# Last block of a fused attention and two-MLP kernel: six tiles of 512 tokens in place of eight of 384, its second product transposed, its buffers laid out anew

## The chip, the cores and the metric

The kernel runs on one core of one Trainium2 chip. The metric is the device time of one execution in microseconds (us). TensorE's clock has two levels, 1.2 and 2.4 GHz; the profile gives the granted level as a share of the higher one (PEclk, 1.0 or 0.5).

## The reference, cut to what matters

Four sequences of 768 tokens, eight heads of 48, pass a linear recurrence with complex decays; its output, 3072 tokens by 384, passes two feed-forward blocks. Only the second of these, the last block, is changed:

```
def _moe_ref(x, w1, w2, w3, w_out):      # 384 -> 1024 -> 384
    return ((x @ w1) * (x @ w2) @ w3) @ w_out

def _moe2_ref(x, w_in, w_out):           # 384 -> 2048 -> 384
    h = x @ w_in
    sp = np.where(h > 20.0, h, np.log1p(np.exp(np.minimum(h, 20.0))))
    g = h * np.tanh(sp)
    return (g @ w_out).astype(np.float32)
```

Everything is float32. On the chip each factor of a large product is split into two float32r parts, hi + lo (`split`: a cast on ScalarE and a subtraction on VectorE), and a product is three matmuls: hi by hi, and the two mixed ones (`mm3`, L464).

## The kernel before, in words

**Ahead of the last block.** The recurrence is done in chunks of 96 tokens, and the first feed-forward block in eight tiles of 384 tokens (`TT`, L28) as generators that `_merge` interleaves (L566 to L579). The first block's result for tile `i` goes to DRAM, transposed, as `x2_d[i]` of 128 x 3 x 384: at the end of `m1_stream` each of three PSUM banks is copied to the buffer `x2`, of which there is one (`bufs=1`, L510), and stored from there (L511, L512). The last tile, `m1_stream(7)`, is drained by itself at L591.

**The last block.** Tokens stay in eight tiles of 384. For each tile and each of 16 slices `f` of the 2048 hidden units:

- `hid` (L601): nine matmuls of 384 columns give the hidden slice in PSUM (128 hidden units by 384 tokens). The stationary operands are the parts of `w_in` (`wih`, `wil`), the moving ones the parts of the tile's input (`x2h`, `x2l`). ScalarE takes sigmoid(-h) to `wb`, VectorE copies h to `hb`. Five PSUM banks go round.
- `soft` (L613): over groups of slices (8 of them, fewer in the first and the last tile), a maximum on VectorE and a logarithm on ScalarE, with a table load ahead of it and one behind it.
- `mish` (L619): for two slices at a time, tanh, the product with `hb`, and the split into `gh` and `gl` (three buffers of each).
- `fin` (L630): nine matmuls accumulate the output of the tile in three PSUM banks. The stationary operands are 128 tokens of `gh` or `gl`, the moving ones a slice of `w_out` (`wuh`, `wul`, 384 columns); a bank holds 128 tokens by 384 outputs.

The loop at L662 runs over all (tile, slice) pairs: `mish` comes 10 steps and `fin` 13 steps behind `hid`, so that in the middle a `hid` and a `fin` of nine matmuls each alternate on TensorE. A tile's input is loaded and split by `x2_load` at slice 8 of the tile before (L676). The first tile's input is loaded at L590, ahead of the last tile of the first block, into buffers of the pool `mp`, which both blocks share; `w_out` comes in 16 slices (`wor`) in the first 16 steps.

The program's order on each engine comes from a scheduler that keeps dependencies; a tile in a buffer that another tile held waits until that one's last reader and its transfers are done. A pool that is opened in the place of closed pools inherits such waits from all that lay there.

```
590    x2_load(0)
591    _drain(m1_stream(NTILE - 1))
592    ph1.close()
594    gp = ph2.enter_context(tc.tile_pool(name="gp", bufs=2))
```

Of the kernel before, what the change touches and what calls it, by code (L numbers as in the profile page):

```python
# [10 lines left out]
F32 = mybir.dt.float32  # L11
# [17 lines left out]
NTILE = NT // TT  # L29
BLK = 7  # L30
EM20 = float(np.exp(-20.0))
# scaled by 2**-112, a float64's leading word holds the float32's exponent; this is the last in its range
# [27 lines left out]
def kernel(  # L60
# [46 lines left out]
    stg = ctx.enter_context(tc.tile_pool(name="stg", bufs=2, side="right"))  # L107
# [7 lines left out]
    # |a| has to lie between 0.75 and 1e4 for the chunked form: 1/|a| within LR of LC  # L115
# [9 lines left out]
    def decode(src, n, dst=None, pool=None, bufs=None, cap=False, signs=False):  # L125
        """float64 words of DRAM to float32 on chip, cut to 24 bits; values out of range are flagged or capped."""
        raw = (pool or stg).tile([128, n, 2], I32, tag="raw64", name="raw64", bufs=bufs)
        if len(src.shape) == 3:
            nc.sync.dma_start(out=raw.rearrange("p (k n) z -> p k (n z)", k=src.shape[1]), in_=src.bitcast(I32))
        else:  # L130
            nc.sync.dma_start(out=raw.rearrange("p n z -> p (n z)"), in_=src.bitcast(I32))
        t = dst if dst is not None else (pool or stg).tile([128, n], I32, tag="dec", name="dec", bufs=2)
        f = t.bitcast(F32)
        i = n_flags[0]
        if not cap:
            n_flags[0] += 1
# [25 lines left out]
    def decode_split(src, hi, lo, step):  # L162
        """Weights as the float32r parts hi + lo, some columns at a time."""
        src, hi, lo = flat(src), flat(hi), flat(lo)
        n = src.shape[1]
        for c0 in range(0, n, step):
            cs = slice(c0, c0 + step)
            split(decode(src[:, cs], step), hi[:, cs], lo[:, cs])
            yield step / 230.0

    def decode_spill(src, dst, step):
        """Weights as float32 in DRAM."""
        src, dst = flat(src), flat(dst)
# [23 lines left out]
    def bh_stream(g):  # L197
        """Decays, their running products and the scaled keys and queries; partitions are (half, head, chunk)."""
# [20 lines left out]
        def norm(i):  # L219
# [19 lines left out]
            # y0 is -2/|a|; within the guarded range 1/(1 + 1e-6/|a|) is 1 - 1e-6/|a| to float32  # L239
# [22 lines left out]
        def steps(i):  # L262
# [5 lines left out]
            for j in range(n):  # L268
# [7 lines left out]
                # [-ai, ar] against Im and [ar, ai] against Re  # L276
# [22 lines left out]
            # from the middle of a chunk to the middle of the next: conj of the decays in between  # L299
# [32 lines left out]
    def ch_stream(g):  # L332
        """A group's chunks in turn: within the chunk, from the state, and the state's update."""
# [38 lines left out]
        def upd(c):  # L372
            """What chunk c adds to the state."""
# [20 lines left out]
        def upd2(c):  # L394
            """The state for chunk c."""
# [75 lines left out]
    def m1_stream(i, before=None):  # L471
        """(x @ w1) * (x @ w2) @ (w3 @ w_out) for a tile of tokens"""
# [109 lines left out]
    def x2_load(i):  # L582
        xh, xl = [mp.tile([128, 3, TT], F32R, tag="x" + z, name="x2" + z) for z in "hl"]
        for kk in range(3):
            raw = mp.tile([128, TT], F32, tag="ul", name="x2r")
            nc.sync.dma_start(out=raw, in_=x2_d[i][:, kk])
            split(raw, xh[:, kk], xl[:, kk])
        x2s[i] = (xh, xl)

    x2_load(0)  # L590
    _drain(m1_stream(NTILE - 1))  # L591
    ph1.close()

    gp = ph2.enter_context(tc.tile_pool(name="gp", bufs=2))
    wuh = gp.tile([128, 16, HD], F32R, name="wuh", bufs=1)
    wul = gp.tile([128, 16, HD], F32R, name="wul", bufs=1)

    GRP = 8
    hw, gg, accs = {}, {}, {}

    def hid(i, f):  # L601
        xh, xl = x2s[i]
        cs = slice(f * 128, (f + 1) * 128)
        if f % GRP == 0:
            hw[i, f // GRP] = [gp.tile([128, GRP, TT], F32, tag=n, name=n) for n in ("hb", "wb")]
        hb, wb = hw[i, f // GRP]
        pool, tag = (mm_p, "mm") if f % 5 < MMB else (at_p, "at")
        ps = pool.tile([128, TT], F32, tag=tag, name="ps_h")
        mm3(ps, [(wih[:, kk, cs], wil[:, kk, cs]) for kk in range(3)], [(xh[:, kk], xl[:, kk]) for kk in range(3)])
        A.activation(out=wb[:, f % GRP], in_=ps, func=AF.Sigmoid, scale=-1.0)  # L610
        V.tensor_copy(hb[:, f % GRP], ps)  # L611

    def soft(i, f0, f1):  # L613
        # -log(sigmoid(-h)) is log(1 + exp(h)); past 20 its tanh is 1
        wb = hw[i, f0 // GRP][1][:, f0 % GRP:f0 % GRP + f1 - f0]
# [3 lines left out]
    def mish(i, f):  # L619
        hb, wb = hw[i, f // GRP]  # L620
        fs = slice(f % GRP, f % GRP + 2)
        A.activation(out=wb[:, fs], in_=wb[:, fs], func=AF.Tanh, scale=-1.0)
        V.tensor_tensor(out=hb[:, fs], in0=hb[:, fs], in1=wb[:, fs], op=mul)
        gh = gp.tile([128, 2, TT], F32R, tag="gh", name="gh", bufs=3)
        gl = gp.tile([128, 2, TT], F32R, tag="gl", name="gl", bufs=3)
        split(hb[:, fs], gh, gl)
# [3 lines left out]
    def fin(i, f):  # L630
        gh, gl = gg.pop((i, f))
        if f == 0:
            accs[i] = [acc_p.tile([128, HD], F32, tag="acc", name="ps_o") for _ in range(3)]
        for m in range(3):
            ms = slice(m * 128, (m + 1) * 128)
            mm3(accs[i][m], [(gh[:, ms], gl[:, ms])], [(wuh[:, f], wul[:, f])], first=(f == 0), final=(f == 15))
        if f == 15:
            for m in range(3):
                osb = mp.tile([128, HD], F32, tag="ul" if m == 1 else "asb", name="osb")
                A.copy(out=osb, in_=accs[i][m])  # L640
                r0 = i * TT + m * 128
                nc.sync.dma_start(out=out[r0:r0 + 128], in_=osb)
            del accs[i]

    def in_range():
        """Whether every decay and every weight lies within the guarded range."""
# [12 lines left out]
    seq = [(i, f) for i in range(NTILE) for f in range(16)]  # L659
    LAG1, LAG2 = GRP + 2, GRP + 5  # L660
    SOFT = {0: [0, 4, 8, 16], NTILE - 1: [0, 8, 14, 16]}
    for n in range(len(seq) + LAG2):  # L662
# [3 lines left out]
        if n < len(seq):  # L666
            i, f = seq[n]
            if i == 0:
                raw = mp.tile([128, HD], F32, tag="uh", name="wor")
# [6 lines left out]
            if f == 8 and i + 1 < NTILE:  # L676
# [5 lines left out]
    ph2.close()  # L682
# [5 lines left out]
def general_path(tc, af, kqf, vf, w1, w2, win, wout, w3o_d, perm, gsum, out, decode):  # L688
    """The recurrence step by step, for inputs whose decays leave the range of the chunked form."""
# [5 lines left out]
    with ExitStack() as st:  # L695
# [57 lines left out]
        with tc.tile_pool(name="g_b", bufs=1) as p, tc.tile_pool(name="g_ps2", bufs=1, space=PSUM) as pp:  # L753
# [17 lines left out]
            with tc.For_i(0, NT, C) as r0:  # L771
# [19 lines left out]
                x2 = p.tile([128, 3, C], F32, name="x2")  # L791
                ps2 = pp.tile([128, 4, C], F32, tag="a", name="ps2")
# [6 lines left out]
                po = pp.tile([C, HD], F32, tag="o", name="po")  # L799
                for g in range(4):  # L800
# [11 lines left out]
                    for j in range(4):  # L812
                        f = g * 4 + j
                        T.matmul(po, lhsT=th[:, j], rhs=wov[:, f], start=(f == 0), stop=(f == 15))
                ob = p.tile([C, HD], F32, name="ob")
                A.copy(out=ob, in_=po)
                nc.sync.dma_start(out=out[bass.ds(r0, C)], in_=ob)


def layout(inputs):  # L820
    i = {k: np.ascontiguousarray(x) for k, x in inputs.items()}
    # token order within a chunk: the first half reversed, then the second half
# [69 lines left out]
```

## Time and profile before

| what | value |
|---|---|
| device time, three runs | 1094.98, 1097.23, 1096.2 us (median 1096.2) |
| profiled execution, first to last instruction (span) | 1098.7 us |
| TensorE busy in matmuls, whole span | 999.2 us, 91% |
| ScalarE, VectorE, GpSimd busy | 712.2, 721.3, 100.0 us |
| last block on TensorE | 692.65 us to the end |
| DMA | 121.10 MB, mean 110 GB/s |

The profiled execution is known by its span alone, which is 2.5 us above the median of the runs. Matmuls are pipelined: a record of a matmul is longer than the distance to the next one, so its price is read from starts, or from a stretch of the chain of waits divided by the matmuls in it. The records' ends are modelled.

### The profile page before, as it was taken

How to read it: one execution, taken by the hardware profiler on the slowest of the kernel's cores; microseconds unless marked ns; L12 is line 12 of the kernel's file. 1: busy time of each engine (PE TensorE's matmuls, PEld its weight loads, DVE VectorE, ACT ScalarE, POOL GpSimd, SP SyncE). 2: the span in 40 equal slices, each digit the busy share in tenths (PEclk: the TensorE clock that was granted, in tenths of full speed). 3: DMA queues.
4: the chain of work that ended last, by engine and by line, in shares of the span. 5: the costliest groups of instructions: out<-in, count | busy, mean ns of one | idle time of the engine just before them, and what ended most of it. 6: DMA issues, size and time to landing. Idle time of an engine off the chain costs nothing.

```text
span 1098.7 us, 18162 instructions
## 1 busy us (share of the span) xinstructions
PE 999.2 (91%) x6762; PEld 962.3 (88%) x6762; DVE 721.3 (66%) x1666; ACT 712.2 (65%) x1458; POOL 100.0 (9%) x164
## 2 busy tenths in 40 slices
PE   0218989988999999999999999999999999999997
PEld 0104769888999999999999999999999999999997
DVE  6997888787698889942665532585555556555453
ACT  7847768666576676543776642796666767666574
POOL 1322121022121222110000000000000000000000
PEclk9658889999699999999999999999999999999999
DMA  8668595557465576532647520411010101010000
GB/s 322 188 178 247 134 263 157 151 167 171 107 160 156 120 195 152 129 94 60 159 136 217 177 85 8 130 51 36 9 36 8 44 1 44 1 44 23 1 22 25
DMA packets 71023, 121.10 MB, mean 110 GB/s; under 512 B 7760, under 2 KB 57744, under 8 KB 69520
## 3 DMA queue, kind: packets, MB, share of 16 engines
q1 hardware_dynamic: 59408, 78.67, 26.2%
q0 software_dynamic: 11520, 41.20, 13.7%
q8 instruction: 55, 0.90, 0.3%
q14 instruction: 40, 0.33, 0.1%
HBM read 81.01 MB, written 34.60 MB: 105 GB/s over the span
## 4 chain that ended last, share of the span: by engine, by line
PE 79%; DMA 7%; DVE 6%; ACT 4%; issue 3%; POOL 0%; SPq 0%; POOLq 0%; DVEq 0%; ACTq 0%
PE ps_o L469 18%; PE ps_h L469 18%; PE pa L469 8%; PE pb L469 8%; PE acc L469 8%; PE ps_a L409 4%; PE ps_u L376 4%; PE ps_y L420 3%; PE ps_tr L361 3%; PE ps_y L419 3%; PE ps_f L189 2%; DMA raw<-in_w3t 1%; DMA ws<-w 1%; DMA raw<-in_a 1%; DMA tm<-kq_d 1%
## 5 line engine op out<-in xcount | busy, mean ns | idle before, releaser
L611 DVE COPY hb<-ps_h 128x384 f32<-128x384 f32 x128 | 69.3, 554 | 125.5 <-ACT wb L610 124.9
L469 PE MATMUL ps_o<-wuh,gh 128*128 128x384 f32 x384 | 128.5, 335 | 0.0
L469 PE MATMUL ps_o<-wul,gh 128*128 128x384 f32 x384 | 128.3, 334 | 0.0
L469 PE MATMUL ps_h<-x2h,wil 128*128 128x384 f32 x384 | 128.3, 334 | 0.0
L469 PE MATMUL ps_h<-x2h,wih 128*128 128x384 f32 x384 | 128.3, 334 | 0.0
L469 PE MATMUL ps_h<-x2l,wih 128*128 128x384 f32 x384 | 128.3, 334 | 0.0
L469 PE MATMUL ps_o<-wuh,gl 128*128 128x384 f32 x384 | 128.0, 334 | 0.0
L189 PE MATMUL ps_f<-wos,dec 128*128 128x384 f32 x128 | 55.8, 590 | 74.0 <-DVE dec L154 74.0
L189 PEld LDWEIGHTS ps_f<-wos,dec 128*128 128x128 f32 x128 | 28.2, 232 | 93.0 <-DVE dec L154 75.2
L610 ACT ACTIVATE wb<-ps_h 128x384 f32<-128x384 f32 x128 | 60.8, 491 | 70.8 <-PE ps_h L469 70.6
L420 PE MATMUL ps_y<-vv,am 96*96 96x48 f32 x512 | 82.3, 251 | 0.0
L121 DVE TENSOR_TENSOR gl<-hb,gh 128x768 fp32r<-128x768 f32 x64 | 61.0, 955 | 30.7 <-ACT gh L120 30.5
L488 DVE TENSOR_TENSOR u<-asb,pb 128x384 f32<-128x384 f32 x64 | 35.2, 551 | 64.9 <-PE pb L469 63.0
L419 PE MATMUL ps_y<-zs,qf 96*96 96x48 f32 x448 | 73.9, 247 | 0.0
L469 PEld LDWEIGHTS ps_o<-wuh,gh 128*128 128x128 f32 x384 | 72.1, 188 | 0.3 <-ACT gh L120 0.3
L469 PE MATMUL pb<-xh,w2h 128*128 128x384 f32 x192 | 68.9, 359 | 3.6 <-ACT asb L484 3.5
L469 PEld LDWEIGHTS ps_h<-x2l,wih 128*128 128x128 f32 x384 | 72.1, 188 | 0.0
L469 PEld LDWEIGHTS ps_h<-x2h,wih 128*128 128x128 f32 x384 | 72.1, 188 | 0.0
L469 PEld LDWEIGHTS ps_o<-wul,gh 128*128 128x128 f32 x384 | 72.1, 188 | 0.0
L469 PEld LDWEIGHTS ps_h<-x2h,wil 128*128 128x128 f32 x384 | 72.1, 188 | 0.0
L469 PEld LDWEIGHTS ps_o<-wuh,gl 128*128 128x128 f32 x384 | 72.0, 188 | 0.0
L469 PE MATMUL pa<-xh,w1h 128*128 128x384 f32 x192 | 69.8, 364 | 1.1 <-ACT xh L437 0.8
(140 smaller groups left out, 2736.4 us busy)
## 6 DMA issues: line engine op xcount, KB each, us to landing
tm<-kq_d SPq DMA_DIRECT2D x64, 288.0 KB, 4.8
raw<-in_a POOLq DMA_DIRECT2D x28, 336.0 KB, 4.3
raw<-in_w3t SPq DMA_DIRECT2D x8, 1024.0 KB, 5.0
kqt<-in_kq POOLq DMA_DIRECT2D x24, 336.0 KB, 5.7
kq_d<-kt POOLq DMA_DIRECT2D x48, 168.0 KB, 4.2
kq_d<-kt POOLq DMA_DIRECT2D x24, 336.0 KB, 3.7
raw<-in_w SPq DMA_DIRECT2D x16, 384.0 KB, 4.4
raw<-in_win SPq DMA_DIRECT2D x12, 512.0 KB, 4.3
```

The source lines that it names most:

```text
L121: V.tensor_tensor(out=lo, in0=raw, in1=hi.bitcast(F32), op=sub)
L189: T.matmul(ps, lhsT=f[:, kk], rhs=wos[:, kk], start=(kk == 0), stop=(kk == 7))
L361: T.transpose(ps[:, hh], tm[c][:, h0 + hh, z], id_sb[0:C, 0:C])
L376: T.matmul(ps[:, h], lhsT=tm[c][:, h, 0], rhs=vt[c][:, h], start=True, stop=True)
L409: T.matmul(ps[:, hh], lhsT=kf[c][:, h], rhs=qf[c][:, h], start=True, stop=True)
L419: T.matmul(ps[:, h], lhsT=qf[c][:, h], rhs=st["z"][:, h], start=True, stop=False)
L420: T.matmul(ps[:, h], lhsT=am[:, h], rhs=vt[c][:, h], start=not inter, stop=True)
L469: T.matmul(ps, lhsT=l, rhs=r, start=first and n == 0, stop=final and n == len(seq) - 1)
L488: V.tensor_tensor(out=u, in0=asb, in1=pb, op=mul)
L610: A.activation(out=wb[:, f % GRP], in_=ps, func=AF.Sigmoid, scale=-1.0)
L611: V.tensor_copy(hb[:, f % GRP], ps)
```

## The change: six tiles of 512, outputs transposed, new pools

1. **Tile.** The last block works on `NT2` = 6 tiles of `T2` = 512 tokens. `hid`'s matmuls have 512 moving columns. There are 6 x 16 x 9 matmuls in `hid` and as many in `fin`, 1728 in all where there were 2304; the columns in sum are the same.
2. **`fin` transposed.** The parts of `w_out` are stationary, `gh` and `gl` move; a bank holds 128 outputs by 512 tokens, and the output in DRAM is 384 x 3072, transposed on the host by an index assignment.
3. **Input.** A tile of 512 lies in two of the blocks of 384 in DRAM, so each of its three parts comes in two transfers.
4. **Buffers.** `hb` goes by pairs of slices (seven buffers), `gh` and `gl` have two buffers where they had three, and `x2r`, `wor` and `osb` share one tag `tmp` with four buffers.
5. **Pools.** `mp` is closed together with the pools of the first block, and `gp`, with everything that the last block uses, is opened in their place; `stg` moves to the side of `mp`. `x2_load(0)` stands behind the last tile of the first block.

The path for decays out of range (`general_path`), which doesn't run with these inputs, is adapted to the transposed output. The core of the diff:

```diff
+T2 = 512
+NT2 = NT // T2
+GRP, XB, GB, HB2 = 8, 2, 2, 7
...
-    stg = ctx.enter_context(tc.tile_pool(name="stg", bufs=2, side="right"))
+    stg = ph1.enter_context(tc.tile_pool(name="stg", bufs=2))
...
     def x2_load(i):
-        xh, xl = [mp.tile([128, 3, TT], F32R, tag="x" + z, name="x2" + z) for z in "hl"]
+        xh, xl = [gp.tile([128, 3, T2], F32R, tag="x" + z, name="x2" + z, bufs=XB) for z in "hl"]
         for kk in range(3):
-            raw = mp.tile([128, TT], F32, tag="ul", name="x2r")
-            nc.sync.dma_start(out=raw, in_=x2_d[i][:, kk])
+            raw = gp.tile([128, T2], F32, tag="tmp", name="x2r", bufs=4)
+            t0 = i * T2
+            while t0 < (i + 1) * T2:
+                j, o = divmod(t0, TT)
+                n = min(TT - o, (i + 1) * T2 - t0)
+                nc.sync.dma_start(out=raw[:, t0 - i * T2:t0 - i * T2 + n], in_=x2_d[j][:, kk, o:o + n])
+                t0 += n
             split(raw, xh[:, kk], xl[:, kk])
...
-    x2_load(0)
     _drain(m1_stream(NTILE - 1))
     ph1.close()
+    ph2.close()
...
-    gp = ph2.enter_context(tc.tile_pool(name="gp", bufs=2))
+    ph3 = ExitStack()
+    gp = ph3.enter_context(tc.tile_pool(name="gp", bufs=2))
     wuh = gp.tile([128, 16, HD], F32R, name="wuh", bufs=1)
     wul = gp.tile([128, 16, HD], F32R, name="wul", bufs=1)
+    x2_load(0)
...
-        gh = gp.tile([128, 2, TT], F32R, tag="gh", name="gh", bufs=3)
-        gl = gp.tile([128, 2, TT], F32R, tag="gl", name="gl", bufs=3)
-        split(hb[:, fs], gh, gl)
+        gh = gp.tile([128, 2, T2], F32R, tag="gh", name="gh", bufs=GB)
+        gl = gp.tile([128, 2, T2], F32R, tag="gl", name="gl", bufs=GB)
+        split(hb, gh, gl)
...
-            accs[i] = [acc_p.tile([128, HD], F32, tag="acc", name="ps_o") for _ in range(3)]
+            accs[i] = [acc_p.tile([128, T2], F32, tag="acc", name="ps_o") for _ in range(3)]
...
-            mm3(accs[i][m], [(gh[:, ms], gl[:, ms])], [(wuh[:, f], wul[:, f])], first=(f == 0), final=(f == 15))
+            mm3(accs[i][m], [(wuh[:, f, ms], wul[:, f, ms])], [(gh, gl)], first=(f == 0), final=(f == 15))
...
-                nc.sync.dma_start(out=out[r0:r0 + 128], in_=osb)
+                nc.sync.dma_start(out=out[m * 128:(m + 1) * 128, i * T2:(i + 1) * T2], in_=osb)
```

On SyncE's queue, where the first block ends: `x_d_77` is the DRAM block of the first block's last tile (`x2_d[7]`), `x_d_70` and `x_d_71` those of its first two, and `x_7896`, `x_7899`, `x_7902` (now `x_7882`, `x_7885`, `x_7888`) the three fillings of the buffer `x2`. Before, with one load of the first tile's input (`x_d_70`) standing some rows ahead of the stores:

```order
L586 DMA x2r<-x_d_70 128x384 x2
L512 DMA x_d_76<-x_7577 128x384
L512 DMA x_d_76<-x_7580 128x384
L586 DMA x2r<-x_d_71 128x384
L670 DMA wor<-wo_d 128x384
L512 DMA x_d_77<-x_7896 128x384
L670 DMA wor<-wo_d 128x384
L586 DMA x2r<-x_d_71 128x384 x2
L670 DMA wor<-wo_d 128x384
L512 DMA x_d_77<-x_7899 128x384
L670 DMA wor<-wo_d 128x384
L586 DMA x2r<-x_d_72 128x384
```

Now, with the semaphores that each row waits for (DMAHW4 is the one that the store of `x_7888` counts up):

```order
L515 DMA x_d_77<-x_7882 128x384 [waits Activation_49]
L515 DMA x_d_77<-x_7885 128x384 [waits DMAHW3_49,Activation_49]
L515 DMA x_d_77<-x_7888 128x384 [waits DMAHW4_49,Activation_49]
L593 DMA x2r<-x_d_70 128x384 [waits DMASW7_49,DMAHW0_49,DMASW6_49,DMAHW1_49,DMASW5_49,DMAHW2_49,DMASW4_49,DMAHW3_49,DMASW3_49,DMAHW4_49,DMASW2_49,DMAHW5_49,DMASW1_49,DMAHW6_49,DMASW0_49,DMAHW7_49,DVE_49,PE_49]
L593 DMA x2r<-x_d_71 128x128
L593 DMA x2r<-x_d_70 128x384
L593 DMA x2r<-x_d_71 128x128
L593 DMA x2r<-x_d_70 128x384
```

The first tile's loads have moved behind all three stores of the first block's last tile, and the first of them waits for every transfer queue, VectorE and TensorE: for the landing of the last store and for the last matmul of the first block.

On ScalarE at the same place, before (`uh` and `acc` belong to the first block, `x2h`, `wuh` and `wb` to the last):

```order
L120 CAST uh<-u 128x384
L511 COPY x_7896<-acc 128x384
L120 CAST x2h<-x2r 128x384
L120 CAST wuh<-wor 128x384
L610 ACT_TABLE_LOAD
L610 ACTIVATE wb<-ps_h 128x384
L511 COPY x_7899<-acc 128x384
```

Now:

```order
L123 CAST uh<-u 128x384
L514 COPY x_7882<-acc 128x384
L514 COPY x_7885<-acc 128x384
L514 COPY x_7888<-acc 128x384
L123 CAST x2h<-x2r 128x512 x3
```

The three casts of the first tile's input, which stood among the work of the first block, now stand behind its last copy.

## Rows read from the trace of the kernel before

**Rows 1.** The page, parts 1 and 2: busy time by engine; granted clock in tenths.

```profile
PE 999.2 (91%) x6762; PEld 962.3 (88%) x6762; DVE 721.3 (66%) x1666; ACT 712.2 (65%) x1458; POOL 100.0 (9%) x164
...
PEclk9658889999699999999999999999999999999999
```

**Rows 2.** Windows in the last block: stretch, length, busy us (instructions) by engine, granted clock, DMA share.

```profile
693.00:1093.00 400.00, 399.76 (x2305) 398.89 (x2304) 226.56 (x312) 272.24 (x374) 0.00 (x0) 1.00 0.10 30
```

**Rows 3.** Chain that ended last, two pieces in the last block: start, length, matmuls.

```profile
692.82 22.88 PE ps_h L469 x132
...
1070.91 21.86 PE ps_o L469 x126
```

**Rows 4.** Timeline of TensorE, clock 1.0: float32 matmuls of 384 columns, two passes a column.

```profile
120.42 1.13 PE L189 MATMUL ps_f<-wos,dec 128*128 128x384 f32 x3
120.74 1.13 PE L189 MATMUL ps_f<-wos,dec 128*128 128x384 f32 x3
121.06 1.13 PE L189 MATMUL ps_f<-wos,dec 128*128 128x384 f32 x3
```

**Rows 5.** Timeline of TensorE, clock 0.5: float32r matmuls of the first block.

```profile
288.39 0.52 PE L469 MATMUL pa<-xh,w1l 128*128 128x384 f32 x1
288.71 0.52 PE L469 MATMUL pa<-xh,w1h 128*128 128x384 f32 x1
289.03 0.52 PE L469 MATMUL pa<-xl,w1h 128*128 128x384 f32 x1
```

**Rows 6.** Weight loads: float32r of the last block by tile, and float32 ones in the timeline.

```profile
L469 PEld LDWEIGHTS ps_h<-x2h,wih x384: 187/188/188, 692.5 to 1070.1; 128*128 128x128 f32 x192
...
147.75 1.44 PEld L376 LDWEIGHTS ps_u<-vv,tm 96*96 96x96 f32 x16
```

**Rows 7.** Timeline of TensorE, ScalarE and SyncE's queue, end of the first block.

```profile
692.48 0.33 PE L469 MATMUL acc<-uh,wol 128*128 128x384 f32 x1
692.65 0.33 PE L469 MATMUL ps_h<-x2h,wih 128*128 128x384 f32 x1
...
691.99 0.48 ACT L511 COPY x<-acc 128x384 f32<-128x384 f32 x1 [1.30 <-PE acc L469]
...
692.49 0.32 SPq L512 DMA_DIRECT2D x_d<-x  x1
```

**Rows 8.** DMA issues: KB each, median us from issue to landing; then the stores' least, median, most.

```profile
x_d<-x SPq DMA_DIRECT2D x24, 192.0 KB, 2.6
x2r<-x_d SPq DMA_DIRECT2D x24, 192.0 KB, 2.5
...
DMA to landing us min/median/max: 1.8/2.6/5.4
```

**Rows 9.** Split of 128 x 512, by tile: duration least/median/most in ns.

```profile
L120 ACT CAST wih<-dec x12: 603/620/660, 523.1 to 579.3; 128x512 fp32r<-128x512 f32 x12
L121 DVE TENSOR_TENSOR wil<-dec,wih x12: 683/691/695, 523.7 to 580.2; 128x512 fp32r<-128x512 f32 x12
```

**Rows 10.** Windows around TensorE's restart after its longest pause; columns as in rows 2.

```profile
72.00:78.00 6.00, 0.00 (x0) 0.00 (x0) 6.00 (x22) 1.14 (x2) 3.13 (x5) 0.50 0.74 194
79.00:84.60 5.60, 5.60 (x9) 2.89 (x9) 5.60 (x13) 3.29 (x6) 1.66 (x3) 0.50 0.90 317
84.80:90.00 5.20, 5.20 (x18) 3.08 (x17) 4.52 (x14) 4.75 (x8) 1.35 (x3) 1.00 0.92 324
```

**Rows 11.** Timeline of VectorE and ScalarE at one logarithm in the last block.

```profile
897.23 1.75 DVE L616 TENSOR_SCALAR wb<-wb 128x3072 f32<-128x3072 f32 x1
...
899.06 1.28 ACT L617 ACT_TABLE_LOAD   x1 [2.33 <-DVE wb L616]
900.35 2.77 ACT L617 ACTIVATE wb<-wb 128x3072 f32<-128x3072 f32 x1
```

**Rows 12.** Groups by line: the split of two slices (busy us, mean ns, idle before).

```profile
L121 DVE TENSOR_TENSOR gl<-hb,gh 128x768 fp32r<-128x768 f32 x64 | 61.0, 955 | 30.7 <-ACT gh L120 30.5
L120 ACT CAST gh<-hb 128x768 fp32r<-128x768 f32 x64 | 53.2, 834 | 18.1 <-PE ps_o L469 18.1
```

More of the change, by code (lines that the diff above doesn't have):

```diff
@@ L582, in x2_load @@
     def x2_load(i):
-        xh, xl = [mp.tile([128, 3, TT], F32R, tag="x" + z, name="x2" + z) for z in "hl"]
+        xh, xl = [gp.tile([128, 3, T2], F32R, tag="x" + z, name="x2" + z, bufs=XB) for z in "hl"]
         for kk in range(3):
-            raw = mp.tile([128, TT], F32, tag="ul", name="x2r")
-            nc.sync.dma_start(out=raw, in_=x2_d[i][:, kk])
+            raw = gp.tile([128, T2], F32, tag="tmp", name="x2r", bufs=4)
[5 more added lines that the diff above has]
+                t0 += n
             split(raw, xh[:, kk], xl[:, kk])
         x2s[i] = (xh, xl)
-    x2_load(0)
     _drain(m1_stream(NTILE - 1))
     ph1.close()
-    gp = ph2.enter_context(tc.tile_pool(name="gp", bufs=2))
+    ph2.close()
+    ph3 = ExitStack()
+    gp = ph3.enter_context(tc.tile_pool(name="gp", bufs=2))
     wuh = gp.tile([128, 16, HD], F32R, name="wuh", bufs=1)
     wul = gp.tile([128, 16, HD], F32R, name="wul", bufs=1)
-    GRP = 8
-    hw, gg, accs = {}, {}, {}
+    x2_load(0)
+    hw, hbs, gg, accs = {}, {}, {}, {}
     def hid(i, f):
@@ L604, in hid @@
         if f % GRP == 0:
-            hw[i, f // GRP] = [gp.tile([128, GRP, TT], F32, tag=n, name=n) for n in ("hb", "wb")]
-        hb, wb = hw[i, f // GRP]
+            hw[i, f // GRP] = gp.tile([128, GRP, T2], F32, tag="wb", name="wb")
+        if f % 2 == 0:
+            hbs[i, f] = gp.tile([128, 2, T2], F32, tag="hb", name="hb", bufs=HB2)
+        hb, wb = hbs[i, f - f % 2], hw[i, f // GRP]
         pool, tag = (mm_p, "mm") if f % 5 < MMB else (at_p, "at")
-        ps = pool.tile([128, TT], F32, tag=tag, name="ps_h")
+        ps = pool.tile([128, T2], F32, tag=tag, name="ps_h")
         mm3(ps, [(wih[:, kk, cs], wil[:, kk, cs]) for kk in range(3)], [(xh[:, kk], xl[:, kk]) for kk in range(3)])
         A.activation(out=wb[:, f % GRP], in_=ps, func=AF.Sigmoid, scale=-1.0)
-        V.tensor_copy(hb[:, f % GRP], ps)
+        V.tensor_copy(hb[:, f % 2], ps)
     def soft(i, f0, f1):
-        wb = hw[i, f0 // GRP][1][:, f0 % GRP:f0 % GRP + f1 - f0]
+        wb = hw[i, f0 // GRP][:, f0 % GRP:f0 % GRP + f1 - f0]
         V.tensor_scalar(out=wb, in0=wb, scalar1=EM20, scalar2=None, op0=ALU.max)
@@ L619, in mish @@
     def mish(i, f):
-        hb, wb = hw[i, f // GRP]
+        hb, wb = hbs.pop((i, f)), hw[i, f // GRP]
         fs = slice(f % GRP, f % GRP + 2)
         A.activation(out=wb[:, fs], in_=wb[:, fs], func=AF.Tanh, scale=-1.0)
-        V.tensor_tensor(out=hb[:, fs], in0=hb[:, fs], in1=wb[:, fs], op=mul)
-        gh = gp.tile([128, 2, TT], F32R, tag="gh", name="gh", bufs=3)
-        gl = gp.tile([128, 2, TT], F32R, tag="gl", name="gl", bufs=3)
-        split(hb[:, fs], gh, gl)
+        V.tensor_tensor(out=hb, in0=hb, in1=wb[:, fs], op=mul)
+        gh = gp.tile([128, 2, T2], F32R, tag="gh", name="gh", bufs=GB)
+        gl = gp.tile([128, 2, T2], F32R, tag="gl", name="gl", bufs=GB)
+        split(hb, gh, gl)
         for z in range(2):
@@ L632, in fin @@
         if f == 0:
-            accs[i] = [acc_p.tile([128, HD], F32, tag="acc", name="ps_o") for _ in range(3)]
+            accs[i] = [acc_p.tile([128, T2], F32, tag="acc", name="ps_o") for _ in range(3)]
         for m in range(3):
             ms = slice(m * 128, (m + 1) * 128)
-            mm3(accs[i][m], [(gh[:, ms], gl[:, ms])], [(wuh[:, f], wul[:, f])], first=(f == 0), final=(f == 15))
+            mm3(accs[i][m], [(wuh[:, f, ms], wul[:, f, ms])], [(gh, gl)], first=(f == 0), final=(f == 15))
         if f == 15:
             for m in range(3):
-                osb = mp.tile([128, HD], F32, tag="ul" if m == 1 else "asb", name="osb")
+                osb = gp.tile([128, T2], F32, tag="tmp", name="osb", bufs=4)
                 A.copy(out=osb, in_=accs[i][m])
-                r0 = i * TT + m * 128
-                nc.sync.dma_start(out=out[r0:r0 + 128], in_=osb)
+                nc.sync.dma_start(out=out[m * 128:(m + 1) * 128, i * T2:(i + 1) * T2], in_=osb)
             del accs[i]
@@ L657, in in_range @@
         return nc.values_load(okt[0:1, 0:1], min_val=0, max_val=1)
-    seq = [(i, f) for i in range(NTILE) for f in range(16)]
+    seq = [(i, f) for i in range(NT2) for f in range(16)]
     LAG1, LAG2 = GRP + 2, GRP + 5
-    SOFT = {0: [0, 4, 8, 16], NTILE - 1: [0, 8, 14, 16]}
+    SOFT = {0: [0, 4, 8, 16], NT2 - 1: [0, 8, 14, 16]}
     for n in range(len(seq) + LAG2):
@@ L668 @@
             if i == 0:
-                raw = mp.tile([128, HD], F32, tag="uh", name="wor")
+                raw = gp.tile([128, HD], F32, tag="tmp", name="wor", bufs=4)
                 nc.sync.dma_start(out=raw, in_=wo2_d[:, f])
@@ L675 @@
                 soft(i, cuts[cuts.index(f + 1) - 1], f + 1)
-            if f == 8 and i + 1 < NTILE:
+            if f == 8 and i + 1 < NT2:
                 x2_load(i + 1)
@@ L681 @@
             fin(*seq[n - LAG2])
-    ph2.close()
+    ph3.close()
     psums.close()
@@ L791, in general_path @@
                 x2 = p.tile([128, 3, C], F32, name="x2")
+                gt = p.tile([128, 16, C], F32, name="gt")
                 ps2 = pp.tile([128, 4, C], F32, tag="a", name="ps2")
@@ L798, in general_path @@
                 V.tensor_copy(x2, ps2[:, 0:3])
-                po = pp.tile([C, HD], F32, tag="o", name="po")
+                po = pp.tile([128, 3, C], F32, tag="o", name="po")
                 for g in range(4):
@@ L811, in general_path @@
                     V.tensor_tensor(out=th, in0=th, in1=ph, op=mul)
[L812 to L815, printed above, removed]
+                    V.tensor_copy(gt[:, g * 4:g * 4 + 4], th)
+                for m in range(3):
+                    for f in range(16):
+                        T.matmul(
+                            po[:, m], lhsT=wov[:, f, m * 128:(m + 1) * 128], rhs=gt[:, f], start=(f == 0), stop=(f == 15)
+                        )
+                ob = p.tile([128, 3, C], F32, name="ob")
                 A.copy(out=ob, in_=po)
-                nc.sync.dma_start(out=out[bass.ds(r0, C)], in_=ob)
+                nc.sync.dma_start(out=out.rearrange("(m p) t -> p m t", p=128)[:, :, bass.ds(r0, C)], in_=ob)
 def layout(inputs):
@@ L881 @@
         args.append(nc.dram_tensor(f"in_{name}", x.shape, mybir.dt.from_np(x.dtype), kind="ExternalInput").ap())
-    args.append(nc.dram_tensor("out_0", (NT, HD), F32, kind="ExternalOutput").ap())
+    args.append(nc.dram_tensor("out_0", (HD, NT), F32, kind="ExternalOutput").ap())
     with tile.TileContext(nc) as tc:
@@ L888 @@
     got = np.asarray(r.results[0]["out_0"])
-    res = np.empty_like(got)
-    res[rows] = got
+    res = np.empty((NT, HD), np.float32)
+    res[rows] = got.T
     return res
```

## Prediction

> **What bounds the kernel now.** I read the page first: TensorE is busy for 91% of the span, no other engine for more than 66%, and the granted clock is at 90% or more in every slice from the twelfth on [rows 1]. That is a mean over stages, so the second view is a window over the last block alone: from 693 to 1093 us TensorE is busy for 399.76 of 400 us at clock 1.0, ScalarE for 272, VectorE for 227 [rows 2]. Nothing but TensorE sets the pace there, and a matmul saved is time saved. The third view, the chain of waits, gives the price of a matmul: 132 of them in 22.88 us and 126 in 21.86 us, 173.3 ns each [rows 3]. 2304 of them make 399.4 us, which is the block. The last view is the timeline where the first block ends: its last matmul starts at 692.48 us and the first of the last block at 692.65 [rows 7]; there is no pause, since the input of the first tile lay ready.
>
> **What a matmul of 512 columns costs.** 384 columns at 2.4 GHz are 160.0 ns, so 13.3 ns of the 173.3 are something else. No row shows 512 moving columns, so I bound it.
>
> - If all 13.3 ns come once a matmul, 512 columns take 213.3 + 13.3 = 226.7 ns, and 1728 of them 391.7 us: 7.7 us less than now.
> - If they grow with the columns, 512 take 231.1 ns and the sum stays 399.4 us.
>
> Which is nearer? A float32 matmul of 384 columns, with the same weight load ahead of each, takes two clock cycles a column, and follows the next at 0.32 us: 120.42, 120.74, 121.06 [rows 4], that is 320 ns and at most a few. At the lower clock float32r matmuls follow each other at 0.32 us too, 384 columns at 1.2 GHz and nothing over [rows 5]. So the extra is neither the price of an instruction nor of a weight load; it shows only where a column passes in one cycle of the faster clock. That is what a limit on the column rate looks like, and such a limit grows with the columns. I take 2.5 ns as fixed (within what rows 4 leave) and 10.8 ns as growing: 2.5 + 512/384 x 170.8 = 230.3 ns, in sum 397.9 us, **1.5 us less**.
>
> The Trainium skill (TensorE: Matmul & The Clock Gate, "Back-to-back issue gap") gives the gap as columns/2.4 plus a fixed 2.5 ns. By it alone the sum would go from 2304 x 162.5 to 1728 x 215.8 ns, 1.5 us less as well. The trace disagrees with it at 384 columns, 173.3 ns [rows 3]; that it holds at 512 is the first rival.
>
> **What the change puts between the blocks.** Before, the first tile's input was loaded and split beside the first block. Now its loads stand on SyncE's queue behind the three stores of that block's last tile, in new buffers, and the first load waits for the landing of the last store; TensorE has nothing else in its order. The chain, from the copies of the first block's output:
>
> - The first copy starts at 691.99 and takes 0.48 us; its store is issued 0.02 us later [rows 7] and lands after 2.6 [rows 8]. The buffer `x2` is single, so the second copy waits for that: 3.1 us a round, three rounds, and the third store has landed at 701.3.
> - Two transfers make one part of the input: 0.4 us to issue the second (a little over the 0.32 of a queue record [rows 7]), 2.5 to landing [rows 8], 0.62 for ScalarE's cast of 512 columns [rows 9]. TensorE's next matmul starts at 704.85, not 692.65: **12.2 us** late.
> - The second matmul needs VectorE's subtraction, 0.69 us [rows 9], while the first takes 0.43 at the lower clock: **0.3 us**. The other two parts follow at the pace of the transfers.
> - The clock falls. After TensorE's longest pause it was at 0.5 with TensorE back at work from 79.0 to 84.6 us, and at 1.0 from 84.8 [rows 10]. Six such us are 14 matmuls of 512 columns at 427 ns in place of 230: **2.8 us**. Ends: 1 us if it rises soon, 4 us if it stays low longer.
>
> With stores at the 1.8 us of the fastest [rows 8], the rounds end 2.4 us earlier; with transfers slower by a fifth, 2 us later. So 10 to 14 us for the pause.
>
> **What stays hidden.** Work on ScalarE and VectorE per column is unchanged, with fewer instructions; they have a third of the block free [rows 2]. The two transfers for a part and the strided input come a tile ahead. `w_out`'s slices arrive behind the first tile's input: ScalarE's sigmoid stands behind two of their casts, but five PSUM banks give TensorE some 10 us of `hid` before it needs one back. If that cover failed, each us would show. Two buffers of `gh` in place of three: a cast must now wait for the `fin` two pairs back, and its result is due two and a half steps later, a step being 18 matmuls or 4.1 us: 10.4 us. Cast and subtraction of 1024 columns take about 2.3 us (0.83 and 0.96 at 768 [rows 12], scaled). Even with a whole logarithm ahead of them on ScalarE (maximum 1.75, load 1.28, logarithm 2.77, by 4/3 without the load [rows 11], 7.3 us) they are done in 9.6. At the end the last copy has 128 columns more, about 0.1 us, and its store a third more bytes: **0.4 us** together. The first 692 us keep their order on all engines: nothing.
>
> **Sum.** 12.2 + 0.3 + 2.8 + 0.4 - 1.5 = 14.2 us more. It is made against the span of 1098.7 us, giving 1112.9; the runs' median is 2.5 us below that span, so I forecast 1096.2 + 14.2 = **1110.4 us**. The change saves TensorE no columns, only matmuls, and buys that with an open seam.
>
> **Rivals.**
>
> - *The extra of a matmul is fixed.* 1728 x 226.7 ns: -7.7 in place of -1.5, so +8.0 us, 1104.2. For it: a price per instruction is the simplest reading of 13.3 ns. Against: rows 4 and 5, where the same instructions don't have it.
> - *Something beside the matmul takes 173 ns, and a longer matmul covers it: faster.* The weight load of the next matmul has a record of 188 ns [rows 6], longer than the 160 of the columns. If it binds, 512 columns take 213.3 + 2.5 = 215.8 ns, 372.9 us in sum: -26.5 + 15.7 = -10.8 us, 1085.4. Against: 16 loads of 96 columns fit into 1.44 us [rows 6], some 0.085 us apart though each record is twice that, so a record's length is not the load's price. The point from which this side decides: the seam and the tail cost 15.7 us, so the change breaks even where 1728 matmuls take 383.7 us, 222.0 ns each. Any fixed price above 8.7 ns over the columns loses.
> - *Two buffers of `gh` are too few.* The margin above is 0.8 us in the worst case. Were TensorE to wait 1 us at each of 14 logarithms, 1124. For it: `gh`'s cast already waits for `fin` with three buffers, 18.1 us in sum [rows 12]. Against: that is ScalarE's idle time, and TensorE lost 0.24 us in 400 [rows 2].
> - *The seam doesn't open.* If the input came in time after all, +15.7 would shrink to about 1 and the time be 1096. Against: the load's wait is in the program.
>
> **Chances.** The forecast 0.55; fixed extra 0.27; covered extra 0.08; waits for `gh` 0.06; no seam 0.04. What a measurement of this kernel can tell from no change is about 0.2%, 2.2 us. Slower: the forecast, the fixed extra and the waits for `gh`, 0.88; faster: the covered extra and a quarter of no seam, 0.09; same: the rest of no seam, 0.03. The forecast's own range is 1106 to 1115 (pause 10 to 14 us, clock 1 to 4, a matmul 230.3 to 231.1). With the fixed extra it reaches down to 1102. 1102 to 1115 leaves out the covered extra, most of the waits for `gh` and the case without a seam.
>
> **What would show it.** Right: no matmul for some 12 us behind the last `acc`, with the loads of `x2r` issued behind the last store's landing; clock 0.5 in that slice; then pieces of the chain that divide to 230 ns a matmul; no idle TensorE elsewhere; the block ending some 14 us later. Wrong: 227 ns or 216 ns a matmul in that division (first or second rival), TensorE idle ahead of `ps_o` behind `gl` (third), or loads that are issued before the stores (fourth).

## The result, and the profile after

The changed kernel takes 1106.3 us (median of 8 runs, 1102.55 to 1109.79), the kernel before 1097.89 (8 runs, 1094.98 to 1105.12): a ratio of 1.0064, 95% interval 1.0038 to 1.0090, some 7 us slower (8.4 by the medians). Forecast were 1110.4 us, 14.2 more than before, and a range of 1102 to 1115. The profiled executions have spans of 1098.7 and 1103.9 us, 5.2 us apart; their parts are taken apart here.

TensorE's part of the page after, where [rows 1] answer:

```profile
PE 994.4 (90%) x6186; PEld 888.1 (80%) x6186; DVE 713.9 (65%) x1592; ACT 694.3 (63%) x1370; POOL 100.0 (9%) x164
...
PEclk9658889999699999999999999899999999999999
```

Two windows of the changed kernel (length, busy us and instructions of TensorE, of its weight loads, VectorE, ScalarE and GpSimd, granted clock, DMA share, GB/s): the seam behind the last matmul of the first block, and the last block with TensorE full, where [rows 2] answer:

```profile
691.60:702.30 10.70, 0.17 (x1) 0.00 (x0) 0.00 (x0) 1.58 (x3) 0.00 (x0) 0.69 0.36 116
711.00:1091.00 380.00, 379.98 (x1677) 314.14 (x1676) 214.90 (x232) 245.53 (x272) 0.00 (x0) 1.00 0.08 26
```

380.00 us hold 1677 matmuls of 512 columns: 226.6 ns each. The chain of work that ended last says it more exactly, with the seam (the passage from the first block to the last) in the same view (start, length, what, count; before: [rows 3]):

```profile
689.98 0.91 PE acc L472 x4
690.89 0.02 issue
690.91 0.49 ACT x L514
691.40 0.02 issue
691.42 1.84 DMA x_d<-x
...
693.36 0.49 ACT x L514
693.85 0.02 issue
693.86 1.87 DMA x_d<-x
...
695.84 0.49 ACT x L514
696.32 0.02 issue
696.34 1.85 DMA x_d<-x
...
698.45 0.32 SPq L593
698.77 0.05 issue
698.82 2.45 DMA x2r<-x_d
...
701.65 0.63 ACT x2h L123
702.28 0.04 issue
702.32 31.03 PE ps_h L472 x126
...
761.91 2.04 PE ps_o L472 x9
763.95 2.04 PE ps_h L472 x9
```

Nine matmuls in 2.04 us are 226.7 ns. Ahead of 702.32 the chain is the predicted one: three rounds of copy and store, the loads of the input, the cast. Besides this pause no matmul is listed with a wait in the block; the list of TensorE's waits from 691 to 1097 us (us in total, times, longest) has one line:

```profile
PE ps_h L472 <- ACT x2h L123: 10.6, 1, 10.6
```

The last matmul of the first block starts at 691.43 us and the first of the last block at 702.32; before, they were 692.48 and 692.65 [rows 7]. The clock is at 0.5 from 695.67 to 705.91 us, and the first eight matmuls take 4.1 us instead of 1.8, as the timeline of the restart shows (start, length, operation, idle before):

```profile
702.32 0.80 PE L472 MATMUL ps_h<-x2h,wih 128*128 128x512 f32 x1 [10.55 <-ACT x2h L123]
703.05 0.80 PE L472 MATMUL ps_h<-x2l,wih 128*128 128x512 f32 x1
703.64 0.63 PE L472 MATMUL ps_h<-x2h,wil 128*128 128x512 f32 x1
704.06 0.63 PE L472 MATMUL ps_h<-x2h,wih 128*128 128x512 f32 x1
704.49 0.63 PE L472 MATMUL ps_h<-x2l,wih 128*128 128x512 f32 x1
704.92 0.63 PE L472 MATMUL ps_h<-x2h,wil 128*128 128x512 f32 x1
705.36 0.74 PE L472 MATMUL ps_h<-x2h,wih 128*128 128x512 f32 x1
706.08 0.50 PE L472 MATMUL ps_h<-x2l,wih 128*128 128x512 f32 x1
706.42 0.40 PE L472 MATMUL ps_h<-x2h,wil 128*128 128x512 f32 x1
```

Not all of these 2.3 us are the clock. The second and the eighth matmul start 0.30 and 0.29 us later than the 0.43 of the lower clock allows; there the weight loads ahead of them wait for VectorE's subtraction:

```profile
703.04 0.29 PEld L472 LDWEIGHTS ps_h<-x2l,wih 128*128 128x128 f32 x1 [0.44 <-DVE x2l L124]
...
706.08 0.19 PEld L472 LDWEIGHTS ps_h<-x2l,wih 128*128 128x128 f32 x1 [0.44 <-DVE x2l L124]
```

The 5.2 us of the two spans, from the starts of matmuls in both timelines: the pause +10.7 (10.89 for 0.17); slow restart and scattered small gaps +2.4 (the block takes 394.66 us for 391.68 of matmuls, before 399.94 for 399.36); width -7.7; from the end of the last matmul to the end of the span +0.8 (6.9 for 6.1); the first block -1.05, which is no effect of the change: in the kernels below that leave its code alone (the change, e1, e2, e5, e6) it ends between 689.22 and 693.32 us.

### The profile page after: what moved, and what is told of

Its sections match the earlier page's. It is cut to its first block, busy times and chain, and to the rows that moved or that the text cites. A ratio compares the mean times of both kernels' runs of the same rounds, so it can differ in the third digit from the quotient of the medians.

```text
span 1103.9 us, 16819 instructions
## 1 busy us (share of the span) xinstructions
PE 994.4 (90%) x6186; PEld 888.1 (80%) x6186; DVE 713.9 (65%) x1592; ACT 694.3 (63%) x1370; POOL 100.0 (9%) x164
## 4 chain that ended last, share of the span: by engine, by line
PE 78%; DMA 8%; DVE 6%; ACT 4%; issue 2%; SPq 1%; POOL 0%; ACTq 0%; DVEq 0%; POOLq 0%
PE ps_h L472 18%; PE ps_o L472 18%; PE pa L472 8%; PE pb L472 8%; PE acc L472 8%; PE ps_u L379 4%; PE ps_a L412 3%; PE ps_tr L364 3%; PE ps_y L423 3%; PE ps_y L422 3%; PE ps_f L192 2%; DMA raw<-in_w3t 2%; DMA x_d<-x 1%; DMA raw<-in_wo 1%; DMA ws<-w 1%
## 5 line engine op out<-in xcount | busy, mean ns | idle before, releaser
L472 PE MATMUL ps_h<-x2h,wih 128*128 128x512 f32 x288 | 113.0, 392 | 10.6 <-ACT x2h L123 10.6
L472 PE MATMUL ps_h<-x2l,wih 128*128 128x512 f32 x288 | 112.8, 392 | 0.0
L472 PE MATMUL ps_h<-x2h,wil 128*128 128x512 f32 x288 | 112.5, 391 | 0.0
L472 PE MATMUL ps_o<-gl,wuh 128*128 128x512 f32 x288 | 112.1, 389 | 0.0
L472 PE MATMUL ps_o<-gh,wul 128*128 128x512 f32 x288 | 112.1, 389 | 0.0
L472 PE MATMUL ps_o<-gh,wuh 128*128 128x512 f32 x288 | 111.8, 389 | 0.0
L282 DVE TENSOR_TENSOR t<-an,p 128x192 f32<-128x192 f32 x192 | 67.6, 352 | 0.2
L472 PE MATMUL acc<-uh,woh 128*128 128x384 f32 x192 | 65.9, 357 | 0.3 <-ACT uh L123 0.3
L472 PE MATMUL pa<-xh,w1l 128*128 128x384 f32 x192 | 66.0, 344 | 0.0
L472 PE MATMUL acc<-ul,woh 128*128 128x384 f32 x192 | 65.4, 341 | 0.2
## 6 DMA issues: line engine op xcount, KB each, us to landing
raw<-in_w SPq DMA_DIRECT2D x16, 384.0 KB, 4.2
```

The source lines that it names most:

```text
L282: V.tensor_tensor(out=t, in0=win2, in1=_bc(pv[:, ::-1], 2, 2), op=mul)
L472: T.matmul(ps, lhsT=l, rhs=r, start=first and n == 0, stop=final and n == len(seq) - 1)
```

## The experiments

Since the first block varies by a few us from one execution to the next, each run is also read inside its trace: from the start of the last `acc` matmul (end of the first block) to the start of the last `ps_o`, with nothing of the first block in it. A ratio is to the runs of the kernel before in the same set (their medians: 1097.89 us for the change, 1100.98 for e1, e3 and e4, 1099.52 for e7 and e8); times of different sets are not compared.

| kernel | last `acc` | first `ps_h` behind it | last `ps_o` | `acc` to `ps_o`, us | ratio to before (95%) |
|---|---|---|---|---|---|
| before | 692.48 | 692.65 | 1092.42 | 399.94 | 1 |
| the change | 691.43 | 702.32 | 1096.76 | 405.33 | 1.0064 (1.0038 to 1.0090) |
| e1, tiles of 384 | 689.22 | 699.56 | 1102.60 | 413.38 | 1.0096 (1.0058 to 1.0134) |
| e2, tiles of 256 | 693.32 | 703.26 | 1124.11 | 430.79 | one run |
| e3, no pause | 693.61 | 693.79 | 1090.65 | 397.04 | 0.9951 (0.9927 to 0.9974) |
| e4, three copy buffers | 682.95 | 690.22 | 1085.76 | 402.81 | 0.9976 (0.9944 to 1.0008) |
| e5, half the weights | 690.54 | 701.19 | 1099.87 | 409.33 | one run |
| e6, TensorE kept busy | 691.13 | 701.84 | 1094.55 | 403.42 | one run |
| e7, e3 and copy buffers | 692.10 | 692.27 | 1084.28 | 392.18 | 0.9878 (0.9849 to 0.9907) |
| e8, before, two copy buffers | 687.87 | 688.04 | 1088.44 | 400.57 | 0.9953 (0.9927 to 0.9980) |

The theory after the result: a matmul costs columns/2.4 GHz and a fixed 13.3 ns, which is the forecast's first rival; the seam costs what its chain shows. Against it stood the forecast's own reading (the extra grows with the columns), a seam priced by something else, and, for where the 13.3 ns come from, the weight load.

**e1_384: the change at the old width.**

```diff
-T2 = 512
+T2 = 384
```

> The changed kernel with one number undone: the last block in 8 tiles of 384 again, all else as changed (late loads, new pools, transposed output). Theory: a matmul costs its columns plus 13.3 ns whatever its length, so the matmuls go back from 226.7 to 173.3 ns each and the block's sum from 391.7 to 399.4 us: 7.7 us slower than the changed kernel, 1.013 to 1.014 of the kernel before, with the pause between the blocks still 10 to 11 us. Rival, the one that the prediction took: the 10.8 ns grow with the columns, so width is worth 1.5 us and the ratio stays 1.007 to 1.008.

The ratio's interval takes in both. The trace decides: from `acc` to `ps_o` 8.05 us longer than with 512, with a pause 0.55 us shorter, so 8.6 us in the block. The widths account for 7.7 (2304 x 173.3 against 1728 x 226.7 ns); two small waits of 0.2 and 0.4 us for `gh` and `gl` lie in the rest. The window of the full stretch (columns as above) holds 2050 matmuls in 355.00 us, 173.2 ns each, `fin` transposed as it is:

```profile
730.00:1085.00 355.00, 355.00 (x2050) 354.72 (x2049) 200.75 (x270) 237.19 (x317) 0.00 (x0) 1.00 0.07 22
```

So the transposition does not change the price of a matmul. The width is worth what the fixed extra says; 1.5 us is excluded.

**e2_256: a third width.** The same edit with 256.

> The changed kernel with tiles of 256 tokens in the last block (12 of them), a third width for the same matmul. Matmuls of 512 start 226.7 ns apart and matmuls of 384 start 173.3 ns apart, in both forms (traces of the change and of the run with tiles of 384). Theory, the 13.3 ns over columns/2.4 GHz are the same for every width: 106.7 + 13.3 = 120.0 ns between starts. The prediction's reading, 2.5 ns fixed and the rest growing with the columns: 106.7 + 2.5 + 7.2 = 116.4 ns. A third way: the weight load, whose record is 188 ns long at every width, becomes the limit, and the starts are further apart than 120 ns. Only starts without a wait between them are read; the time of the whole is of no interest here.

The window of the full stretch, columns as above, holds 3085 matmuls in 370.00 us, 119.9 ns each:

```profile
740.00:1110.00 370.00, 370.00 (x3085) 369.83 (x3084) 212.03 (x397) 267.29 (x470) 0.00 (x0) 1.00 0.08 23
```

Most starts in the timeline are 120 ns apart. So 106.7 + 13.3, 160.0 + 13.3 and 213.3 + 13.3: the extra is the same at three widths. Weight loads with 188-ns records follow each other at 120 ns here, so their record's length did not set the pace either.

**e5_half_weights: is it the weight load?**

```diff
-            ms = slice(m * 128, (m + 1) * 128)
-            mm3(accs[i][m], ...
+            w = 128 if f in (0, 15) else 64
+            ms = slice(m * 128, m * 128 + w)
+            mm3(accs[i][m][0:w], ...
```

> The changed kernel in which the output matmuls of 14 of the 16 slices hold only 64 columns of weights instead of 128, with the same 512 columns streamed (half of their outputs are left out). If the 13.3 ns between matmuls are the price of loading a block of 128 columns of weights, these matmuls start about 220 ns apart (half of 13.3). If they belong to the matmul itself, whatever it holds, they start 226.7 ns apart as now.

The records of the loads shrink (count: least/median/most ns), the pace does not (window in the full stretch, `hid` and `fin` together: 1485 matmuls in 340.00 us, 229.0 ns):

```profile
L472 PEld LDWEIGHTS ps_o<-gh,wuh x240: 132/134/188, 761.1 to 1079.6; 128*64 128x64 f32 x105, 128*128 128x128 f32 x15
...
740.00:1080.00 340.00, 340.00 (x1485) 242.32 (x1483) 185.86 (x193) 211.47 (x228) 0.00 (x0) 1.00 0.06 20
```

Half the weights save nothing. The 2 ns more are not theirs alone: by the starts in this window the halved matmuls are 230.1 ns apart, the whole ones of `hid` 228.9. The extra is not in proportion to the weights loaded. A fixed price of each weight load is not excluded, since in every run each matmul has a load of its own; what the extra is inside TensorE stays open.

**e3_seam384: the pause taken away.** The input tiles of both blocks share a pool that outlives the first block, the first load goes back ahead of the last tile, and the weights of the last block are decoded 384 columns at a time, which frees the memory for it.

```diff
+    mpx = phx.enter_context(tc.tile_pool(name="mpx", bufs=2))
...
-        xh, xl = [gp.tile([128, 3, T2], F32R, tag="x" + z, name="x2" + z, bufs=XB) for z in "hl"]
+        xh, xl = [mpx.tile([128, 3, T2], F32R, tag="x" + z, name="x2" + z) for z in "hl"]
...
+    x2_load(0)
     _drain(m1_stream(NTILE - 1))
...
-    x2_load(0)
```

> The pause alone undone: six tiles of 512 as changed, but the input tiles stand in a pool that outlives the first block, so that the first tile is loaded and split beside the last tile of the first block. To make room the weights of the last block are decoded 384 columns at a time where they were 512 (12 pieces become 16, beside matmuls). Theory: the pause and the slow first matmuls go (10.7 and 2.3 us), the gain of the wider matmuls (7.7 us) stays: first ps_h within 0.3 us of the last acc, 1089 to 1092 us, ratio to the kernel before 0.992 to 0.995. Rival: the pause only moves, because ScalarE's first sigmoid writes to a buffer of the new pool and waits for the last store; five PSUM banks are then filled and TensorE stops some 10 us into the block for 2 to 6 us: ratio 0.997 to 1.000.

The pause is gone: `ps_h` follows `acc` after 0.18 us, and the clock stays up there. This kernel beats the kernel before and the change. 0.9951 lies at the edge of the theory's range, and its interval takes in the rival's 0.997 as well, so the trace has to decide. `acc` to `ps_o` is 8.3 us shorter than in the change, not the 13 of pause and restart: one wait took 2.8 us back, with a fall of the clock to 0.5 behind it (727.8 to 731.2 us). List of TensorE's waits from 690 to 1095 us, and two lines of ScalarE at the seam:

```profile
PE ps_h L474 <- DVE hb L630: 2.8, 1, 2.8
PE ps_o L474 <- ACT gh L125: 0.4, 1, 0.4
```

```profile
697.98 0.48 ACT L516 COPY x<-acc 128x384 f32<-128x384 f32 x1 [1.96 <-DMA x_d<-x]
...
700.48 1.28 ACT L629 ACT_TABLE_LOAD   x1 [2.02 <-DMA x_d<-x]
```

ScalarE goes on with the three copies, each but the first behind a store, until 698.46 us, and the table load ahead of its first sigmoid waits for a store too, until 700.48, some 7 us into the last block. From there it is behind with sigmoids and casts, and behind the matmul of 723.58 TensorE finds no free PSUM bank. So both had a part: the pause is gone, as the theory said, and a stall of the rival's kind and size came, though 30 us into the block and not 10. e7 tests this reading.

**e4_x2bufs: the seam's first half alone.** The copies get three buffers, so that the stores needn't wait for each other.

```diff
-            x2 = mp.tile([128, TT], F32, tag="x2", name="x2", bufs=1)
+            x2 = mp.tile([128, TT], F32, tag="x2", name="x2", bufs=3)
```

> The changed kernel with three buffers for x2, the copy of the first block's output, where it has one. Theory: the pause is three rounds of copy and store, one behind the other; with three buffers the copies follow the matmuls at once and the stores overlap, the last lands near 694.5 us instead of 698.4, and the pause shrinks from 10.7 to about 6.5 us: 4 us faster than the changed kernel, ratio to the kernel before 1.002 to 1.004. Rival: the first load waits for something else in the list of its waits (an earlier transfer, a drain of the pool), and the pause stays above 10 us, ratio 1.006.

The pause falls from 10.89 to 7.27 us, so the rounds of copy and store were 3.6 us of it. `acc` to `ps_o` gains only 2.5 of them: the clock stays at 0.5 until some 6 us behind the first `ps_h`, where the change had it for 3.6, so the price of a restart is not the same in these two.

```profile
690.30:696.10 5.80, 5.80 (x12) 3.68 (x13) 3.07 (x6) 4.21 (x7) 0.00 (x0) 0.50 0.67 208
```

The gain by the ratios is larger, 1.0064 to 0.9976, some 10 us (5 to 14 by the two intervals). (The 7.7 us that e7's expectation names is the difference of two medians from different sets, in which the kernel before differed by 3.1 us.) The rest lies ahead of 682.95 us, inside the first block, which neither theory had. e8 looks at that alone.

**e6_warm: the clock alone.** 44 matmuls that nothing reads fill TensorE's pause.

```diff
+    pd = acc_p.tile([128, T2], F32, tag="acc", name="ps_d")
+    for k in range(44):
+        T.matmul(pd, lhsT=wih[:, 0, 0:128], rhs=wih[:, 0, 0:T2], start=(k == 0), stop=(k == 43))
```

> The changed kernel with 44 more matmuls of 512 columns in the pause, whose result nobody reads, so that TensorE's clock does not fall. Theory: the first eight matmuls of the block are set by the arrival of the input's three parts (casts at 701.7, 702.6 and 704.7 us, the last subtraction done at 706.0), not by the clock: the granted clock stays 1.0, the second to eighth matmul wait for x2h and x2l, and the ninth starts at the same distance from the last acc, within 0.5 us. Rival, the prediction's separate 2.8 us for the clock: the ninth matmul starts 2 us earlier and the span is 2 us shorter.

Windows of the pause and of the 4 us behind it: the clock stays at 1.0, and 16 records fall where the change had 8.

```profile
691.60:701.80 10.20, 9.87 (x44) 7.83 (x42) 0.00 (x0) 1.58 (x3) 0.00 (x0) 1.00 0.37 118
701.80:705.80 4.00, 3.96 (x16) 2.82 (x17) 2.63 (x5) 2.30 (x5) 0.00 (x0) 1.00 0.64 196
```

`acc` to `ps_o` is 1.9 us shorter, 0.2 of it in the pause. So the theory falls and the rival comes near: the arrival of the input did not set the restart alone, the clock cost about 1.7 us of the 2.4. One caution: in this run TensorE's order at the start takes matmuls of several slices in turn, which may hide part of the wait for the third piece of the input.

**e7_best: no pause, and no copy that waits.** e3, with two of the three copies in the buffers `asb`.

```diff
-            x2 = mp.tile([128, TT], F32, tag="x2", name="x2", bufs=1)
+            x2 = mp.tile([128, TT], F32, tag="asb" if m else "x2", name="x2", bufs=None if m else 1)
```

> The run without the pause (input tiles shared by both blocks, weights in pieces of 384), in which two of the three copies that the first block stores per tile go to buffers of another tile, so that no copy waits for a store. The run of the change with three copy buffers gained about 7.7 us where the pause alone gave 3.6. Theory, the other 4 us came from copies inside the first block that no longer hold ScalarE up: this kernel is another 3 to 4 us faster than the one without the pause (0.9951), a ratio of 0.991 to 0.993. Rival, those 4 us were variation from run to run: 0.994 to 0.996.

Better than the theory: 0.9878, the best of all kernels here. Three matmuls of `ps_h` were done ahead, so 1725 x 226.7 = 391.0 us is the least from `acc` to `ps_o`; it takes 392.18. TensorE's list of waits from 690 to 1095 us, and two lines of ScalarE at the seam:

```profile
PE ps_o L474 <- ACT gh L125: 0.2, 1, 0.2
```

```profile
691.58 1.42 ACT L516 COPY x<-acc 128x384 f32<-128x384 f32 x3 [1.30 <-PE acc L474]
695.54 1.28 ACT L629 ACT_TABLE_LOAD   x1 [2.53 <-DMA x_d<-x]
```

The three copies now follow each other without a wait. The table load still waits for a store, but it starts 3.3 us into the last block, where e3 had it after 6.7, and e3's stall is gone. So of the 0.73% between e3 and e7, 4.9 us lie in the last block (397.04 to 392.18); the theory had looked for its 3 to 4 us in the first block, where about 3 are left by the ratios, with an uncertainty as large. Against e8, in the same set, 0.9878/0.9953 is 0.75%, 8.2 us, with some 4 us of uncertainty by the two intervals; in the traces the last block is 7.8 us shorter than before (392.18 for 399.94). That is what the width is worth (7.7) when nothing is paid for it.

**e8_before_x2: the first block's share.** The kernel before with `bufs=2` in the line of e4.

> The kernel before with two buffers instead of one for the copies that the first block stores, and nothing else. It has no pause between the blocks, so a gain can only come from inside the first block. Theory (ScalarE is held up by the single buffer): 2 to 4 us faster, a ratio of 0.996 to 0.998. Rival (those waits are covered by other work of TensorE): no change, 0.999 to 1.001.

0.9953 (0.9927 to 0.9980): the single buffer costs the kernel before some 5 us, a little over the theory, whose range the interval takes in. The part of the last block is unchanged (400.57 for 399.94 us). The tiles of the first block end at 236.7, 320.2, 390.5 and 455.6 us before, at 238.6, 316.7, 384.0 and 450.8 here: in these two executions the gain falls in the second and third tile, then mostly stays. Windows of 236 to 320 us, before and here, and from the lists of waits in that stretch TensorE's for the copy `asb` and ScalarE's for the stores, before and here:

```profile
236.00:320.00 84.00, 75.72 (x540) 72.49 (x539) 63.35 (x196) 51.95 (x136) 17.47 (x28) 0.90 0.63 153
```

```profile
236.00:320.00 84.00, 77.80 (x584) 74.59 (x584) 68.81 (x221) 55.59 (x144) 17.48 (x28) 0.94 0.67 159
```

```profile
PE pb L469 <- ACT asb L484: 3.5, 2, 3.0
...
ACT x L511 <- DMA x_d<-x: 6.1, 2, 4.0
```

```profile
PE pb L469 <- ACT asb L484: 0.6, 1, 0.6
...
ACT x L511 <- DMA x_d<-x: 1.9, 1, 1.9
```

Before, ScalarE is held up to 4.0 us by a store and TensorE up to 3.0 us by ScalarE's copy `asb`; with the second buffer both shrink, and TensorE's mean clock in the stretch is 0.94 for 0.90. That the one wait sets the other is read from the two lists, not tried by itself. The buffer also changed the scheduler's order in those tiles; the runs do not tell the order and the wait apart.

## Why the prediction was right or wrong

The side and the range held; the likeliest case did not come, the first rival did (1104.2 us), and the range had been drawn to take it in. That the median of 1106.3 also lies inside the forecast's own 1106 to 1115 is luck, since that range rests on a price of a matmul that was wrong. By the forecast's own terms:

- **Width: wrong.** The step that failed is "I take 2.5 ns as fixed [...] and 10.8 ns as growing". It argued from matmuls that lack the extra (two cycles a column, or the lower clock) that the extra is a limit on the column rate, and so grows with the columns. But these matmuls only showed where the extra does not appear, not how it scales. Measured: 226.7 ns, 7.7 us saved instead of 1.5; e1 and e2 give the same 13.3 ns at 384 and 256 columns. The rule of the Trainium skill (TensorE: Matmul & The Clock Gate, "Back-to-back issue gap"), which that section gives for the isolated gap of a single matmul, a fixed sum over the columns, has the right form, but not the size for this stream: 13.3 ns where it has 2.5. The prediction called the rule's holding at 512 its first rival; by the rule's 215.8 ns it is the second, and had the matmuls of 512 started that far apart, beside the measured 173.3 at 384, the change would have won. The Trainium skill's gap for the lower clock in the same section, columns/1.2 GHz, is what the restart shows (0.43 us for 512).
- **Pause: right, 1.5 us too long.** 10.7 us for 12.2. The stores landed 1.84 to 1.87 us after issue, near the least of [rows 8] and not at its median of 2.6: 2.45 us a round for 3.1, 2.0 us less in all. Against it the chain from the store's landing to the first matmul took 4.1 us, where I had 3.5 (four short steps on SyncE's queue ahead of the load, 0.26 us in all, and 0.32 us of issue ahead of the cast). That the pause is this chain, e3 and e4 show: without the late loads it is gone, with overlapping stores it is 3.6 us shorter.
- **Restart and clock: right, a little too dear.** 2.4 us for 0.3 + 2.8. The wait for the first subtraction was 0.30 us, as forecast. The clock stayed low for seven of the block's matmuls, 3.6 us, where the forecast had 14 in some six us; e6 gives its share as about 1.7 us.
- **What stays hidden: right.** The one line of waits leaves no room for `gh`, the casts of `w_out` or the strided input; the third rival fell. In e1 and e3 such waits appear, 0.2 to 0.4 us for `gh` and `gl` and 2.8 for a PSUM bank, so the margin is thin where ScalarE is behind.
- **Tail: 0.8 us for 0.4.** It is near the spread of that stretch: from the last `ps_o` to the end of the span the kernel before takes 6.28 us, e8 with the same code there 6.86, the change 7.14.
- **The sum.** 10.7 + 2.4 + 0.8 - 7.7 = 6.2 us where 14.2 was forecast; 6.2 of the 8.0 us between are the width, 1.5 the pause, 0.7 the restart, and the tail goes 0.4 the other way.
- **The second rival** (a covered extra, 215.8 ns) is excluded by the same division. Its break-even of 222.0 ns a matmul becomes 223.1 with the measured 13.9 us of seam and tail; at 226.7 the change loses, and with the seam's cost taken out, in e3 and e7, the same width wins.

## What to carry to other kernels

Price a wider matmul by both readings of its overhead, growing with the columns and fixed for each instruction, and count the price of the buffers it needs: here 7.7 us of fewer matmuls were a real gain, and moving the first load behind a pool's close cost 13. When pools are laid out anew, look first at the loads that used to be ahead of the seam; a pool that outlives it, and copies that have a buffer each, kept the gain (e7). And a single buffer between a copy and its store made the copying engine wait for each landing ahead of the next copy (2.45 us a round at the seam); what queues behind that engine can pay for it, as TensorE did in e3.

## What the runs showed of the hardware that was not expected

- float32r matmuls with a weight load each start columns/2.4 GHz + 13.3 ns apart at clock 1.0, for 256, 384 and 512 columns (120.0, 173.3, 226.7 ns). At clock 0.5 there is nothing over: 512 columns take 0.43 us in the restart above (703.64 to 704.92, three distances), 512/1.2 = 427 ns, as 384 take 0.32 [rows 5].
- The extra does not shrink with half the weight columns (229.0 ns in e5), and loads whose records are 188 ns long follow each other every 120 ns (e2).
- Two buffers in place of one for a copy that is stored gained 0.47% (0.20 to 0.73) in a kernel whose TensorE is busy 91% of the span.
